# RWKV6 attention and an MLP mixer in one kernel: another written sequence for the whole program, and where the u-weighted grams of the first three units are masked

## The chip, the cores and the metric

The kernel runs on 1 core of one Trainium2 chip. The metric is the device time of one execution in microseconds (us). Three runs of the kernel before took 481.3, 478.45 and 478.63 us, the median is 478.63. The page and the trace show one further execution, which the hardware profiler took; its own time is given below.

## The reference

Attention in the RWKV6 form with batch 4, 8 heads, 768 steps and head size 48, then an MLP mixer over tokens (768 to 256 to 768) and over channels (384 to 1536 to 384). Everything is float32.

```
for t in range(S):                       # per batch and head, state is 48x48
    cur = outer(u * k[t], v[t])
    y[t] = r[t] @ (state + cur)
    state = w[t][:, None] * state + outer(k[t], v[t])

x = y as (4, 768, 384)
h = relu(x.T @ w_tok1) @ w_tok2          # over tokens
u = x + h.T
out = u + relu(u @ w_ch1) @ w_ch2        # over channels
```

## The kernel before

**Units.** The 768 steps of a batch are cut into 12 chunks of 64 (T), two chunks to a block of 128 rows, two blocks to a unit: three units per batch (UB), 12 units in all, 0 to 11. Units 0 to 2 are batch 0. A unit works through these pieces: `ends` (a scan on VectorE, DVE, over w, L435, into `to_end`), two range checks on ScalarE (ACT) that only set flags (L427, a pass over `to_end` into a tile `junk`), `keys` (L440), `begins` and `queries` (L443, L446), `tokens` (PE transposes the keys, L345, and ACT copies them, L350), `carry` (L365, outer products of keys and values), four state steps, each a scaling on ACT (`by`, L501, four instructions of two heads each) and an addition (`up`; in batch 0 a product by the identity on PE, L508, later on DVE, L516), `gram` (products of queries and keys inside a chunk), `mask` (L327, a masked copy from PSUM into the tile `at`), then `before` with `across` (L380, queries times the state), `seen` (L389 in the start, L392 later: ACT reads one column of the banks that `across` has filled), `after` with `within` (L401, `at` times values, added in the same banks, so it comes after `seen`) and `taken` (L407, ACT moves the result into the mixer's input).

**The u part.** The term `u * k` at a step itself needs the diagonal of a gram whose keys were scaled by u. In the first batch each unit makes it so: `own_u` scales the keys on ACT (L331), `own_gram` multiplies on PE (L315, into the two PSUM halves `gram`), and `own_put` on DVE multiplies the result by a mask of ones on the diagonal into `at`:

```
def own_put():
    for q, g in L.pop("own"):
        dve.tensor_mul(at[:, q], g, over_heads(on_diagonal, g.shape[1]))
```

`mask` of the same unit then writes the strictly lower part over it, so it must come after. Unit 3 does the same once for all later batches, whose units take that part by other means.

**Weights.** All four weight matrices arrive as 32-bit words and are converted piece by piece, 8 pieces in all: load, `plus` and `minus` on ACT (L264, L267), `lead` (L270), `two` (L273), `value` (L277) and `sum` (L281) on DVE. The first three pieces are the token weights, the others the channel weights `wch`.

**Mixer.** Batch 0 is mixed with the float32 weights directly: `hidden` (L947 and L669 in the exact form), `back` (L958), `turn` (a transpose, L969, copied by L974), up products (L993), down products (L1004). Batches 1 to 3 go through an exact scheme of split numbers: up products in three passes L772, L774 and L779, z by L754, L757 and L761 (ACT, ACT, DVE, with an addition L765 on GpSimd, POOL), and down products in three passes L790, L791 and L792. This needs the weights split: for the channel weights `up_part` on ACT (L579), `rest` on DVE (L583), `low_part` on ACT (L586), `store` of the parts into DRAM (L594), read back through a ring of SBUF buffers by `load_third` (L626). z shares its room with `wch`, from which the six stores of the up weights read. The tiles `spare` and `h_room` hold token weights in turn: `tok1_moves` (L704) writes what lies in them to DRAM (`kept`) and reloads it; `weight_form` (L711, L715) derives parts of them, `row_form` (L689) puts the mixer's rows there. `kept0` (L921) and `kept1` (L828) load the token weights of the next batch back from what was written.

**Order.** Nothing is left to a scheduler: every piece is a function, and PE, DVE, ACT and SP (whose queue issues most DMAs) take their instructions in the order in which the functions are called. For the start (units 0 to 2, the token weights, hidden layer of batch 0) that order is one long call `strict(...)` of functions; `behind(gate, f)` lets a load wait for the piece `gate`. The remainder is woven by `ORDER`, a string of digits: each digit takes the next piece of one of ten lists (0 the mixings, 1 and 2 joins and token parts, 3 hidden parts, 4 to 6 the units by i modulo 3, 7 loads, 8 the channel weights' conversion and splits, 9 the second hidden half):

```
pieces = interleaved(ORDER, first_mixing() + of_mixing[0], *of_mixing[1:4], *of_units, loads, weights_in_turn(), of_mixing[4])
```

Of the kernel before, what the change touches and what calls it, by code (L numbers as in the profile page):

```python
# [18 lines left out]
ALU = mybir.AluOpType  # L19
# [4 lines left out]
T = 64  # L24
C = S // 128
UC = 2
UB = C // UC
NU = B * UB
A = H // 2
# [20 lines left out]
MID = 3 * G // 4 * SEG1  # L50
ORDER = (
    "888008088078808800000888484440800840804080880808804844088488400448088408008888080080884808884040488844488888084840880880"
    "808840880808084448484008800080858808005000458500505588854545558485085848785005080558505855588400558085800005606068606846"
    "860600685786865658688606668086688566668868066800064869889466550048096660988848898089000484488044008000848080000018444141"
    "404040044004000000007000000404000440020000040550000050500000000000000005024200200045005020000555542000002004001224540105"
    "100550500055000750000000055050502000000500004500006624606000520000666506507606600506566660066600060066066606000000000000"
    "006405041104010500004006511611111661096012294296211041111044222990403443439223340234000004000010011000000400000007040000"
    "400040004004000400400000404000055000550000000000000000000005544000050000000000500014511000000000400000004555500545554000"
    "570550000450000000505550060000600066000506665000000665005600000000000066500001666656650661160651610000600006662106266212"
    "191166106100991111112002023393229933300002000001000110000000000000000000000000000000000000000000000000000000000000000000"  # L60
    "00000000000070001011000000000000000000000000000000000000000000000000000000000000000000000000000000000"
# [4 lines left out]
def rwkv6_then_mixer(  # L66
# [255 lines left out]
    def over_heads(mask, n=2):  # L322
        return mask.unsqueeze(1).unsqueeze(1).to_broadcast([128, n, X, T])
# [85 lines left out]
    def unit(i):  # L409
# [46 lines left out]
        def own_put():  # L456
            for q, g in L.pop("own"):
                dve.tensor_mul(at[:, q], g, over_heads(on_diagonal, g.shape[1]))
# [74 lines left out]
        def each(f, n):  # L533
            return [lambda m=m: f(m) for m in range(n)]

        return dict(ranges=each(ranges, 2), ends=ends, keys=keys, begins=begins, queries=queries, own_u=each(own_u, A),
# [481 lines left out]
    def attention_pieces(i):  # L1018
# [21 lines left out]
        small, large = (piece(e["ranges"][n], name, ("ACT", 1.4, k("ends"))) for n, name in enumerate(("small", "large")))  # L1040
# [34 lines left out]
    def interleaved(order, *streams):  # L1075
# [12 lines left out]
    e0, e1, e2 = (unit(i) for i in range(UB))  # L1088
    (_, p0, n0, lead0, two0, put0, add0), (_, p1, n1, lead1, two1, put1, add1), (_, p2, n2, lead2, two2, put2, add2) = to_tok
    _, p3, n3, lead3, two3, put3, _ = to_ch[0]  # L1090
    in_turn.update({pe.engine: None, dve.engine: None, act.engine: None, sp.engine: None})
    s0, s1, s2 = (e["updates"] for e in (e0, e1, e2))
    t0, t1, t2 = (e["scaled"] for e in (e0, e1, e2))
    strict(lambda: load_part(0, 1), masks, e0["ends"], e0["own_u"][0], e0["own_u"][1], e0["own_u"][2], e0["own_u"][3], e0["begins"],
           lambda: load_part(0, 0), e0["keys"], lambda: load_part(1, 1), e0["own_gram"], lambda: load_v(0), e0["ranges"][0], lambda: load_w(1),
           e0["tokens"], e0["queries"], e1["own_u"][0], e1["own_u"][1], e0["copied"][0], lambda: load_w(2), e0["gram"], e1["ends"], e0["copied"][1],
           lambda: load_part(1, 0), e0["carry"], e1["own_u"][2], s0[0], e0["own_put"], e1["own_u"][3], e0["ranges"][1], t0[1], s0[1],
# [248 lines left out]
```

## Time and profile before

| | us |
|---|---|
| median of three runs | 478.63 |
| the profiled execution, its own time | 478.31 |
| its span, first to last instruction | 476.5 |
| PE, matrix products, busy | 459.1 (96%) |
| PEld, weight loads of PE (beside products) | 409.6 (86%) |
| DVE busy | 344.6 (72%) |
| ACT busy | 265.8 (56%) |
| POOL busy | 54.2 (11%) |

The DMAs moved 85.34 MB, 179 GB/s in the mean. The granted clock of PE was 1.0 over the whole span.

Each row of a group names a line of the kernel, an engine, an operation, output<-input, and then a count and times. `L458` is line 458 of the kernel before. A bracket at a row's end, `[0.59 <-ACT raw L267]`, is the idle time of that engine ahead of the instruction and what ended it. Rows of the stretch view begin with from:to in us from the span's start. `SPq` is SP's DMA queue; a DMA row's last number is the median time from issue to landing. The numbers behind a slash, as in 1162/1194/1225, are the shortest, the mean and the longest duration in ns.

### The profile page before, as it was taken

How to read it: one execution, taken by the hardware profiler on the slowest of the kernel's cores; microseconds unless marked ns; L12 is line 12 of the kernel's file. 1: busy time of each engine (PE TensorE's matmuls, PEld its weight loads, DVE VectorE, ACT ScalarE, POOL GpSimd, SP SyncE). 2: the span in 40 equal slices, each digit the busy share in tenths (PEclk: the TensorE clock that was granted, in tenths of full speed). 3: DMA queues.
4: the chain of work that ended last, by engine and by line, in shares of the span. 5: the costliest groups of instructions: out<-in, count | busy, mean ns of one | idle time of the engine just before them, and what ended most of it. 6: DMA issues, size and time to landing. Idle time of an engine off the chain costs nothing.

```text
span 476.5 us, 12778 instructions
## 1 busy us (share of the span) xinstructions
PE 459.1 (96%) x5322; PEld 409.6 (86%) x5322; DVE 344.6 (72%) x495; ACT 265.8 (56%) x606; POOL 54.2 (11%) x58
## 2 busy tenths in 40 slices
PE   3899999999999999999999999999999999999996
PEld 2776588856797668999999999999999999999995
DVE  7998797679598877876897998685587885235341
ACT  6699876674678856453747385351837554134140
POOL 1000000000000001231302002130304003032130
PEclk9999999999999999999999999999999999999999
DMA  8865745573584556963888842754784513336331
GB/s 313 317 221 217 188 169 191 180 275 99 152 228 138 177 179 207 284 186 100 252 283 232 294 154 56 198 173 141 215 227 150 167 61 84 115 101 199 86 99 54
DMA packets 45055, 85.34 MB, mean 179 GB/s; under 512 B 4736, under 2 KB 37376, under 8 KB 44992
## 3 DMA queue, kind: packets, MB, share of 16 engines
q1 hardware_dynamic: 44704, 84.37, 56.3%
q8 instruction: 43, 0.70, 0.6%
q14 instruction: 20, 0.16, 0.1%
q10 hardware_dynamic: 288, 0.10, 0.1%
HBM read 72.65 MB, written 11.80 MB: 177 GB/s over the span
## 4 chain that ended last, share of the span: by engine, by line
PE 90%; ACT 4%; DVE 2%; DMA 2%; issue 1%; SPq 0%; DVEq 0%; ACTq 0%
PE bank L1004 10%; PE bank L772 8%; PE bank L779 8%; PE bank L774 8%; PE bank L790 8%; PE bank L792 8%; PE bank L791 8%; PE bank L993 7%; PE bank L667 3%; PE bank L989 3%; PE bank L726 3%; PE bank L315 2%; PE bank L401 2%; PE bank L380 2%; PE kv_ps L365 2%; PE bank L669 2%
## 5 line engine op out<-in xcount | busy, mean ns | idle before, releaser
L765 POOL TENSOR_TENSOR z_high<-z_high 128x384 fp32r<-128x384 f32 x48 | 52.9, 1107 | 406.7 <-DMA ring<-third 186.8
L754 ACT ACTIVATE z_high<-bank 128x384 fp32r<-128x384 f32 x48 | 23.5, 489 | 58.1 <-PE bank L779 57.7
L772 PE MATMUL bank<-x_forms,forms 128*128 128x384 f32 x216 | 50.3, 341 | 0.0
L779 PE MATMUL bank<-z_more,forms 128*128 128x384 f32 x216 | 50.1, 340 | 0.0
L774 PE MATMUL bank<-x_forms,ring 128*128 128x384 f32 x216 | 49.3, 337 | 0.0
L761 DVE SCALAR_TENSOR_TENSOR z_high<-bank,z_high 128x384 fp32r<-128x384 f32 x48 | 26.5, 554 | 31.4 <-ACT z_high L754 29.4
L1004 PE MATMUL bank<-wch,z 128*128 128x384 f32 x144 | 48.1, 488 | 0.0
L790 PE MATMUL bank<-forms,z_high 128*128 128x384 f32 x140 | 47.8, 342 | 0.0
L792 PE MATMUL bank<-forms,z_high 128*128 128x384 f32 x140 | 47.1, 337 | 0.0
L791 PE MATMUL bank<-ring,z_high 128*128 128x384 f32 x140 | 47.1, 337 | 0.0
L798 DVE SCALAR_TENSOR_TENSOR x<-bank,x 128x384 f32<-128x384 f32 x35 | 18.8, 553 | 39.0 <-PE bank L792 38.9
L1004 PEld LDWEIGHTS bank<-wch,z 128*128 128x128 f32 x144 | 26.8, 190 | 17.2
L501 ACT ACTIVATE before<-state,to_end 112x48 f32<-112x48 f32 x132 | 33.1, 324 | 13.0 <-DVE state L516 7.6
L779 PEld LDWEIGHTS bank<-z_more,forms 128*128 128x128 f32 x216 | 39.0, 188 | 0.1
L772 PEld LDWEIGHTS bank<-x_forms,forms 128*128 128x128 f32 x216 | 38.3, 188 | 0.5
L774 PEld LDWEIGHTS bank<-x_forms,ring 128*128 128x128 f32 x216 | 38.6, 188 | 0.0
L993 PE MATMUL bank<-xT,wch 128*128 128x256 f32 x144 | 32.0, 381 | 0.0
L993 PEld LDWEIGHTS bank<-xT,wch 128*128 128x128 f32 x144 | 27.0, 190 | 3.7
L757 ACT ACTIVATE z_high<-z_high 128x384 fp32r<-128x384 f32 x48 | 25.2, 525 | 3.5
L790 PEld LDWEIGHTS bank<-forms,z_high 128*128 128x128 f32 x140 | 26.3, 188 | 0.2
L791 PEld LDWEIGHTS bank<-ring,z_high 128*128 128x128 f32 x140 | 26.3, 188 | 0.0
L792 PEld LDWEIGHTS bank<-forms,z_high 128*128 128x128 f32 x140 | 26.3, 188 | 0.0
(243 smaller groups left out, 961.2 us busy)
## 6 DMA issues: line engine op xcount, KB each, us to landing
ring<-third SPq DMA_DIRECT2D x144, 192.0 KB, 3.4
raw<-in_words_ch_dram SPq DMA_DIRECT2D x8, 1023.8 KB, 4.8
rk<-in_rk_dram SPq DMA_DIRECT2D x36, 192.0 KB, 5.2
near<-in_near_dram SPq DMA_DIRECT2D x8, 768.0 KB, 5.0
w<-in_w_dram SPq DMA_DIRECT2D x10, 520.5 KB, 5.1
vt<-in_v_dram SPq DMA_DIRECT2D x12, 384.0 KB, 5.0
out_dram<-x SPq DMA_DIRECT2D x17, 192.0 KB, 2.8
third<-forms SPq DMA_DIRECT2D x12, 192.0 KB, 3.3
```

The source lines that it names most:

```text
L501: act.mul(t[:ROWS, a], state[bt, g][:ROWS, a], by_last(c, j)[:, a:a + 1])
L757: act.mul(z_form(jt, 2), z_form(jt, 0).bitcast(f32), 1.0 / BASE)
L761: dve.scalar_tensor_tensor(z_form(jt, 1), a, 0.0, z_form(jt, 0).bitcast(f32), op0=ALU.max, op1=ALU.subtract)
L765: pool.tensor_add(z_form(jt, 2), z_form(jt, 2).bitcast(f32), z_form(jt, 1).bitcast(f32))
L772: pe.matmul(a, up[m], xf(0)[:, m], start=m == 0, stop=False)
L774: pe.matmul(a, low[:, m], xf(1)[:, m], start=False, stop=False)
L779: pe.matmul(banks["a", jt], joint, xf(2)[:, m], start=False, stop=m == 2)
L790: pe.matmul(a, z[0], up, start=first, stop=False, skip_group_check=True)
L791: pe.matmul(a, z[1], held[bt, s, half, 1, jt], start=False, stop=False, skip_group_check=True)
L792: pe.matmul(a, z[2], joint, start=False, stop=last, skip_group_check=True)
L993: pe.matmul(ps, now["wch1"][:, jt // 4, m, ts(jt % 4, 128)], xT[:, m, ts(s, SEG)], start=(m == 0), stop=(m == DM // 128 - 1))
L1004: pe.matmul(ps, zs[s][:, jt, ts(n, 128)], now["wch2"][:, jt, :], start=(jt == 0), stop=(jt == NJ - 1))
```

## The change

Two things are changed, and both parts of the written order with them.

1. In units 0 to 2 `own_put` no longer multiplies on DVE. ACT copies each half of the gram from PSUM into `at`, and GpSimd then sets everything off the diagonal to zero there, in two `affine_select`s, one for each chunk of 64 rows. `mask` still comes after. Unit 3 keeps the multiplication.
2. The long call of the start is replaced by a string `FIRST` of names, which is read out in a loop (`0.own` is `own_gram`, `0.put` is `own_put`, `t0.load` the load of the first piece, `h0` a hidden product, `a<b` is `behind(b, a)`). It is another sequence of the same pieces. `ORDER` is replaced by another string, which gives another interleaving of the same lists.

```diff
+FIRST = (
+    "masks k0 0.own0 0.own1 0.own2 0.own3 r0 0.own 0.ends 0.small 0.large k1 1.own0 0.keys 0.begins 0.tokens 0.copied1 0.queries w1 v0 "
...
+    "2.up2 2.by3 t2.minus h3 2.before 2.seen c0.load<1.gram h5 t2.plus rk3 2.mask 2.after 2.taken1 h7 2.taken0 h4 h6 t1.sum 2.taken2 h9 "
+    "t2.lead t2.two t2.value c0.plus t2.sum c0.minus c0.lead c0.two c0.value c1.load<2.own c2.load<1.tokens h8 h11 h10 relu1 relu0 back0 "
+    "1.large 2.small 1.small 2.large w3<2.by3 v3"
+)
 ORDER = (
-    "888008088078808800000888484440800840804080880808804844088488400448088408008888080080884808884040488844488888084840880880"
...
+    "007888888888008088000088008404448888848808804008880008888000444444444888888880000444484840880448880004884484400080884500005"
...
@@
         def own_put():
             for q, g in L.pop("own"):
-                dve.tensor_mul(at[:, q], g, over_heads(on_diagonal, g.shape[1]))
+                if i < UB:
+                    act.copy(at[:, q], g)
+                    for j in range(2):
+                        of = at[ts(j, T), q]
+                        pool.affine_select(out=of, in_=of, compare_op=ALU.is_equal, fill=0.0, base=0,
+                                           pattern=[[0, 2], [0, X], [1, T]], channel_multiplier=-1)
+                else:
+                    dve.tensor_mul(at[:, q], g, over_heads(on_diagonal, g.shape[1]))
@@
-    strict(lambda: load_part(0, 1), masks, e0["ends"], e0["own_u"][0], e0["own_u"][1], e0["own_u"][2], e0["own_u"][3], e0["begins"],
...
-           h[10], add2, n3, behind(e1["tokens"], to_ch[2][0]), lead3, two3, rectified[0], h[9], h[11], rectified[1], e1["ranges"][0], e2["ranges"][1], e1["ranges"][1],
-           lambda: load_rk(3), put3, lambda: turned["back"](0))
...
+    for name in FIRST.split():
+        name, _, gate = name.partition("<")
+        strict(behind(named[gate], named[name]) if gate else named[name])
```

The lines of the changed kernel stand 11 lower than before up to about line 455 and 18 lower after that: L754 becomes L772, L711 L729, L594 L612, L626 L644, L392 L403, L401 L412.

What the new strings move is shown at three places, each before and with the change, the third on two engines.

**ACT, first z of batch 1 and the reloaded token weights** (z_high and z_more are parts of z, spare and h_room the reloaded tiles). Before:

```order
L754 ACTIVATE z_more<-bank_874 128x384
L754 ACTIVATE z_more<-bank_878 128x384
L501 ACTIVATE before<-state,to_end_93 112x48 x4
L427 ACTIVATE junk,flags<-to_end_93,least 112x1041
L754 ACTIVATE z_high<-bank_877 128x384
L757 ACTIVATE z_high<-z_high 128x384
L754 ACTIVATE z_high<-bank_874 128x384
L757 ACTIVATE z_high<-z_high 128x384
L754 ACTIVATE z_high<-bank_878 128x384
L757 ACTIVATE z_high<-z_high 128x384
L711 ACTIVATE spare<-spare 128x768
L711 ACTIVATE spare<-h_room 128x768
```

With the change:

```order
L772 ACTIVATE z_high<-bank_879 128x384
L775 ACTIVATE z_high<-z_high 128x384
L772 ACTIVATE z_more<-bank_882 128x384
L729 ACTIVATE spare<-spare 128x768
L729 ACTIVATE spare<-h_room 128x768
L519 ACTIVATE before<-state,to_end_93 112x48 x4
L772 ACTIVATE z_more<-bank_881 128x384
L519 ACTIVATE before<-state,to_end_93 112x48 x4
L733 ACTIVATE spare<-spare 128x768
```

The first two z_more rows before are the fifth and the sixth column of the first half. Both uses of the reloaded tiles (L711, now L729) stood behind the sixth and eight more rows of z and state; now they stand right behind the fifth column's z_more and ahead of the sixth's (z_more<-bank_881), with two rows of state scalings (L519) about it.

**SP, the six stores of the up weights** (third<-wch are the stores, ring<-third the loads of parts stored earlier). Before:

```order
L594 DMA third_3_140<-wch_127 128x2x384
L594 DMA third_4_141<-wch_127 128x2x384
L626 DMA ring_2005<-third_0_131 128x384 x2
L626 DMA ring_2005<-third_1_132 128x384 x2
L181 DMA w_90<-in_w_dram 128x1041
L594 DMA third_5_142<-wch_127 128x2x384
L626 DMA ring_2050<-third_2_133 128x384 x2
L626 DMA ring_2050<-third_0_137 128x384 x2
L626 DMA ring_2055<-third_1_138 128x384 x2
```

With the change:

```order
L612 DMA third_3_140<-wch_127 128x2x384
L644 DMA ring_1997<-third_0_131 128x384 x2
L644 DMA ring_1997<-third_1_132 128x384 x2
L612 DMA third_4_141<-wch_127 128x2x384
L192 DMA w_90<-in_w_dram 128x1041
L644 DMA ring_2059<-third_2_133 128x384 x2
L644 DMA ring_2059<-third_0_137 128x384 x2
L644 DMA ring_2064<-third_1_138 128x384 x2
L612 DMA third_5_142<-wch_127 128x2x384
L212 DMA vt<-in_v_dram 128x2x384
```

The sixth store (third_5) stood ahead of the loads of third_2_133, third_0_137 and third_1_138; now it stands behind these three rows of two loads each.

**DVE, the last conversion piece and unit 4** (wch is the converted weight; to_end_93 and rk_89 belong to unit 4, at_92 to unit 3). Before, beginning with the last piece's `lead`:

```order
L270 TENSOR_TENSOR raw<-raw 128x1024
L273 TENSOR_SCALAR raw<-raw 128x1024
L514 COPY state<-kv_ps 112x192
L277 SCALAR_TENSOR_TENSOR wch_127<-raw 128x1024
L281 TENSOR_TENSOR wch_127<-wch_127,raw 128x1024
L583 TENSOR_TENSOR forms_1208<-wch_126,forms_1208 128x768 x2
L516 TENSOR_TENSOR state<-before,kv_ps 112x192
L583 TENSOR_TENSOR forms_1208<-wch_126,forms_1208 128x768 x2
L327 COPY_PREDICATED at_92<-before_it,bank_877 128x512
L327 COPY_PREDICATED at_92<-before_it,bank_875 128x512
```

With the change:

```order
L338 COPY_PREDICATED at_92<-before_it,bank_883 128x512
L338 COPY_PREDICATED at_92<-before_it,bank_884 128x512
L281 TENSOR_TENSOR raw<-raw 128x1024
L534 TENSOR_TENSOR state<-before,kv_ps 112x192
L284 TENSOR_SCALAR raw<-raw 128x1024
L288 SCALAR_TENSOR_TENSOR wch_127<-raw 128x1024
L292 TENSOR_TENSOR wch_127<-wch_127,raw 128x1024
L442 MEMSET starts 112x17
L446 SCALAR_TENSOR_TENSOR to_end_93<-w_90,starts 112x1041
L447 RECIPROCAL starts<-to_end_93 112x16
L451 TENSOR_TENSOR rk_89<-rk_89,to_end_93 112x1024
L281 TENSOR_TENSOR raw<-raw 128x1024
```

Unit 3's mask (L327, now L338) stood behind the last conversion (L270 to L281) and its `rest` rows (L583); now it stands ahead of the conversion before that one, and unit 4's `ends` (L442 to L447) and `keys` (L451), which before followed later, stand ahead of the last conversion, whose `lead` is the last row here.

**ACT, the same place: `seen` of unit 3.** Before:

```order
L427 ACTIVATE junk,flags<-to_end_93,least 112x1041
L350 COPY kT<-bank_878 128x384
L350 COPY kT<-bank_873 128x384
L601 ACTIVATE forms_1208<-forms_1208 128x768
L586 ACTIVATE forms_1256<-forms_1208 128x768
L392 COPY seen<-bank_876 128x1
L392 COPY seen<-bank_874 128x1
```

With the change:

```order
L275 ACTIVATE raw<-raw,rebias 128x1024
L278 ACTIVATE raw<-raw,rebias 128x1024
L597 ACTIVATE forms_1242<-wch_126 128x768 x2
L438 ACTIVATE junk,flags<-to_end_93,least 112x1041
L403 COPY seen<-bank_880 128x1
L403 COPY seen<-bank_881 128x1
```

`seen` (L392, now L403) stood behind the third split of the weights (`low_part` L586, joining L601) and the copied keys; now it stands right behind the last conversion's `plus` and `minus` (L275, L278), two `up_part` (L597) and a range check (L438).

55 lines of the change are left out of this document (26 added, 29 removed), and 5 rows, old and new, of the table FIRST.

## The prediction

> **What bounds the kernel now.** I read the page's head first, then busy time by stretch, then what the matmul engine waits for once the start is over.
>
> ```profile
> span 476.5 us, 12778 instructions
> 6.00:48.00 42.00, 36.88 (x993) 28.96 (x994) 37.70 (x38) 33.89 (x89) 0.00 (x0) 1.00 0.76 276
> 48.00:60.00 12.00, 11.41 (x45) 6.86 (x44) 8.90 (x13) 10.88 (x17) 0.00 (x0) 1.00 0.73 175
> 60.00:180.00 120.00, 120.00 (x1276) 89.84 (x1275) 97.22 (x121) 81.78 (x174) 0.00 (x0) 1.00 0.55 180
> 212.00:290.00 78.00, 77.27 (x1118) 74.92 (x1117) 65.28 (x99) 45.04 (x110) 10.34 (x10) 1.00 0.67 205
> PE bank L969 <- ACT raw L267: 0.6, 1, 0.6
> PE bank L401 <- ACT seen L392: 0.6, 2, 0.3
> PE bank L401 <- issue: 0.5, 1, 0.5
> ```
>
> The columns of a stretch are its length, then busy time of PE, PE's weight loads, DVE, ACT and POOL. The last three rows are all of PE's waits from 58 us to the end. Two regimes show. Up to 48 us DVE (37.70 of 42) and ACT (33.89) set the pace, and from 48 to 60 ACT does (10.88 of 12). From 58 us on PE is full: its waits add up to 1.7 us in 418. So after 58 us the new order can win at most 1.7 us, and every microsecond by which something reaches PE late is added to the end, since no idle time is left in which to make it up. The sum below is made on the profiled execution, 478.3 us with a span of 476.5; the runs' median is 478.63. About 1%, or 4.8 us, is what a measurement of this kernel tells from no change.
>
> **The grams, units 0 to 2.** Three DVE multiplies go; ACT gains three copies of 128x1024 out of PSUM, GpSimd gains six selects of 64x1024.
>
> ```profile
> L458 DVE TENSOR_TENSOR at<-gram,u_rows x2: 1162/1194/1225, 13.9 to 28.5; 128x1024 f32<-128x1024 f32 x2
> 3.57 1.02 ACT L231 ACTIVATE kv_ps<-ident 32x1024 f32<-32x1024 f32 x1
> L223 POOL TENSOR_SCALAR_AFFINE_SELECT strictly<-strictly x2: 232/234/237, 1.4 to 1.7; 64x64 f32<-64x64 f32 x2
> masks.py:199 POOL TENSOR_SCALAR_AFFINE_SELECT ident<-ident 128x128 f32<-128x128 f32 x1 | 0.3, 293 | 0.0
> L765 POOL TENSOR_TENSOR z_high<-z_high x48: 1000/1014/2002, 188.7 to 460.6; 128x384 fp32r<-128x384 f32 x48
> ```
>
> DVE loses 3 x 1.2 = 3.6 us. An ACT instruction over 1024 columns took 1.02, so ACT gains 3 x 1.0 to 1.2, about 3.4. DVE falls from 37.7 to 34.1 and ACT rises from 33.9 to 37.3: the longer of the two is as long as before, and I cost this at 0. Its cover is ACT's free time in the first 48 us (8 us); without that it costs the whole 3.4, and if ACT's load does not count, it wins the 3.6 of DVE. The select has no row of its size. Its two rows differ by 59 ns for 64 more columns, so 1024 columns make 234 + 960 x 0.92 = 1.1 us, a pair 2.2; scaled from the two-input add (2.6 ns a column at 1014) a pair is 5.4. I take 2.2, since it is the same operation. In the new order DVE's masked copy of the unit waits for the pair, with the scan of unit 1 ahead of it as cover, so 2.2 costs nothing and anything beyond about 2.5 delays DVE.
>
> The longest L765 took 2002 against 1014 ns, so something on this chip can double a GpSimd instruction here. [...]
>
> **Hand-over at 48 to 60 us.** ACT now runs all four range checks (L427) in a row behind the second rectified hidden tile and ahead of the conversion of the next weights; before there were three.
>
> ```profile
> 50.90 1.17 ACT L427 ACTIVATE junk<-first,most 112x1041 uint8<-112x1041 f32 x1
> 52.19 1.17 ACT L427 ACTIVATE junk<-to_end,most 112x1041 uint8<-112x1041 f32 x1
> 58.72 0.52 PE L969 MATMUL bank<-ident,x 128*128 128x128 f32 x3 [0.59 <-ACT raw L267]
> ```
>
> One more is 52.19 - 50.90 = 1.3 us, on the chain conversion, DVE, x, transpose, for which PE already waits. Between 0 and 1.3; I take 0.9, as the hidden layer may end a little earlier.
>
> **Unit 3's attention, moved forward.** Its `across` and `within` stood on PE behind 40 down products of the first mixing; now 8 stand ahead of it and 6 between the two. `within` needs `seen` on ACT, which now stands behind two `up_part` (L579) and a range check. Those need the last weights' conversion, and on DVE unit 4's `ends` and `keys` and unit 3's mask have been moved ahead of that.
>
> ```profile
> 94.24 15.64 PE L1004 MATMUL bank<-wch,z 128*128 128x384 f32 x48
> 98.25 0.69 DVE L270 TENSOR_TENSOR raw<-raw 128x1024 int16<-128x1024 int16 x1 [1.87 <-ACT raw L267]
> 100.83 1.23 DVE L281 TENSOR_TENSOR wch<-wch,raw 128x1024 f32<-128x1024 f32 x1
> 102.15 3.78 ACT L579 ACTIVATE forms<-wch 128x768 fp32r<-128x768 f32 x5 [1.44 <-DVE wch L281]
> 106.78 1.33 DVE L327 COPY_PREDICATED at<-before_it,bank 128x512 f32<-128x512 uint8 x2
> 114.55 2.33 DVE L435 TENSOR_TENSOR_SCAN to_end<-w,starts 112x1041 f32<-112x1041 f32 x1
> 117.08 1.16 DVE L440 TENSOR_TENSOR rk<-rk,to_end 112x1024 f32<-112x1024 f32 x1
> 120.70 0.93 PE L345 MATMUL bank<-ident,rk 112*128 112x112 f32 x8
> 122.86 0.96 PE L380 MATMUL bank<-before,rk 48*64 48x48 f32 x42
> ```
>
> On the clock of before: ahead of 98.25 come 2.33 + 1.16 + 0.2 = 3.7 and 1.33, less the idle 1.87 that they fill, so +1.8 (the mask hidden too) to +3.1. The conversion then ends at 103.9 to 105.2 instead of 102.06. Two L579 at 3.78/5 = 0.76, a check of 1.17 and the copy put `seen` at 106.8 to 108.1. PE comes to `within` after 14 x 15.64/24 = 9.1 and the blocks L380 and L345 with 1.9: 105.2, or 106.1 with the 0.9 of the hand-over. It waits between 0.7 and 2.9; I take 1.5.
>
> **The last store of the up weights.** The first z of batch 1 (L754) writes where the six stores read from, so it needs the sixth landed. That store now stands on SP's queue behind six ring loads, which wait for the end of the last `back`; before it stood ahead of them.
>
> ```profile
> 183.52 3.17 SPq L626 DMA_DIRECT2D ring<-third  x7
> third<-wch SPq DMA_DIRECT2D x6, 384.0 KB, 3.3
> third<-wch SPq DMA_DIRECT2D x1, 384.0 KB, 5.6
> ```
>
> The second row is the median of the six stores, the third the one at 150 to 153 us with loads in front. Six issues at 3.17/7 = 0.45 put the store at 186.3, landed at 189.6 to 191.9. The first z takes 0.5 on ACT and 0.55 on DVE until its bank is free: 190.7 to 193.0. PE goes on with other columns and asks for that bank at the fifth: the sixth column ends at 194.84 (next fence: 194.30 + 0.54), a column takes 3 x 0.53 = 1.6, so the fifth begins at 191.7. Stall 0 to 1.3; I take 0.8.
>
> **The reload of the first token weights, bt 2.** SP issues the two reloads (L704) right behind the ring load of batch 1's sixth column; on ACT both uses (L711) and four state scalings now stand between the fifth and the sixth z. Before, ten ACT rows and 14 us lay between issue and use.
>
> ```profile
> 194.30 0.70 PE L779 MATMUL bank<-z_more,forms 128*128 128x384 f32 x3
> 195.43 1.00 ACT L501 ACTIVATE before<-state,to_end 112x48 f32<-112x48 f32 x4
> 200.08 0.34 PE L790 MATMUL bank<-forms,z_more 128*128 128x384 f32 x1
> 210.21 0.83 ACT L711 ACTIVATE spare<-spare 128x768 fp32r<-128x768 f32 x1
> spare<-kept SPq DMA_DIRECT2D x1, 384.0 KB, 7.0
> h_room<-kept SPq DMA_DIRECT2D x1, 384.0 KB, 7.3
> ```
>
> The ring load goes when L774 is done (194.3), the reloads at 194.8 and 195.2. With their own 7.3 the second lands at 202.5; L711 0.83, scalings 1.0 and the z 0.5 make 204.8. PE needs the sixth z ten products later, at 200.08: 4.7 late. With the 3.3 of a store of that size it is 0.6. I take 2.6, the middle, since what is in flight there (ring loads) is as before, but fewer.
>
> **The two write-backs and reloads, bt 1 to 2.** The write-backs of the token weights' low parts (L704), which stood 25 us ahead, now stand in one row with the loads `kept0` and `kept1`, which must wait for them. On ACT the first row form (L689), which overwrites what is written back, stands ahead of the sixth z, and L711 of the second weights ahead of `seen`.
>
> ```profile
> 262.63 0.68 PE L779 MATMUL bank<-z_more,forms 128*128 128x384 f32 x3
> 272.64 1.15 PE L380 MATMUL bank<-before,rk 48*64 48x48 f32 x64
> 264.09 0.54 ACT L689 ACTIVATE spare<-x 128x384 fp32r<-128x384 f32 x1
> kept<-spare SPq DMA_DIRECT2D x1, 384.0 KB, 6.1
> kept<-h_room SPq DMA_DIRECT2D x1, 384.0 KB, 7.9
> z_more<-kept SPq DMA_DIRECT2D x2, 384.0 KB, 7.4
> ```
>
> Write-backs at 263.1 and 263.6. The first landed (6.1) at 269.2, row form and z give 270.2, needed at 262.63 + 5.78 = 268.4: 1.8; with 3.3, none. The second landed at 271.5, `kept1` issued by 272.4 and landed by 279.8, two L711, one L715 and a row form: `seen` at 282.0. PE asks at 272.64 + 1.15 and six L667 (1.0): 274.8, so 7.2 late at the most, counting the 1.8; with 3.3 for each transfer 273.4, not late. I take 2.5 for both, nearer to the short end, since 6.1 to 7.9 are among the longest of their size.
>
> **Sum.** 0 + 0.9 + 1.5 + 0.8 + 2.6 + 2.5 = 8.3: 478.3 + 8.3 = 486.6 us, slower by 1.7%.
>
> **Rivals.** (1) *The transfers land in time.* At the short ends the terms are 0, 0.7, 0, 0.6, 0 and the hand-over 0: 1.3, or 479.6; up to 483.4 it is within 1%. For it: most stores took 3.3 or less. Against it: the four reload and write-back rows lie at 6.1 to 7.9. (2) *Faster.* If DVE alone sets the pace of the first 48 us, its 3.6 us are won in full, and if in addition the later PE waits (1.7) go and no transfer is late, 478.3 - 5.3 = 473.0. This decides when ACT's added 3.4 us fall into its 8 us of idle time and the places above cost less than 0.8 in sum. For it: 37.70 against 33.89; against it: three separate chains above would each have to be wrong. (3) *GpSimd at half speed.* Pairs of 4.3 to 5.4 us make DVE wait some 2 to 3 us in the start; with the terms above 486.6 + 2.5 = 489.1.
>
> **How the numbers follow.** The forecast 0.58, rival 1 0.22, rival 2 0.04 (0.03 of it beyond 1%), rival 3 0.16. Slower by over 1%: 0.58 + 0.16 = 0.74; within 1% 0.23; faster 0.03. The range goes from the middle of rival 1's lower half, 480.0, to 492.5: 6 above the forecast, as the long ends sum to 1.3 + 2.9 + 1.3 + 4.7 + 7.2 = 17.4, which can't all be reached, because a late PE makes the next transfer less late.
>
> **What would show it.** In the profile after: PE busy share down from 96%, with PE waits after 58 us of some 8 us instead of 1.7; PE waiting at the down product (line 808 there) behind ACT near 205 to 210 us, and ACT waiting for DMA at line 729; `within` (line 412) waiting for `seen` near 107; the four checks in a row ending near 54. Selects near 1.1 us, DVE's masked copies not waiting for POOL. Wrong it would be if ACT nowhere waits for a reload, or if the transposes at 59 us come earlier than 58.7 by more than 2 us.

## The result and the profile after

The changed kernel took 497.23 us in the median of four runs (495.62 to 502.51), the kernel before 478.54: a ratio of 1.0403, 95% interval 1.0307 to 1.0498. Forecast were 486.6 us and a range up to 492.5. The direction was right, the loss is more than twice as large. The profiled execution is the slowest of the four, 502.51 us with a span of 500.8, so the places below add up to some 24 us, not to the median's 18.7.

The head of the page and the granted clock in 40 slices:

```profile
span 500.8 us, 12788 instructions
PE 472.4 (94%) x5322; PEld 418.4 (84%) x5322; DVE 344.3 (69%) x492; ACT 269.6 (54%) x609; POOL 67.2 (13%) x64
PEclk9998999999999999989899979999999999999999
```

PE is idle for 28 us instead of 17, and it is also *busy* for 13.3 us more, with the same 5322 products. The clock row shows one source: in four places it is not 9. Finer stretches show how low it went (the third number from the right is the clock):

```profile
44.00:46.00 2.00, 2.00 (x34) 0.92 (x33) 1.79 (x3) 1.98 (x5) 0.00 (x0) 0.50 0.76 197
214.00:216.00 2.00, 2.00 (x8) 2.00 (x7) 1.97 (x4) 0.79 (x4) 0.00 (x0) 0.50 0.04 5
246.00:248.00 2.00, 2.00 (x8) 2.00 (x8) 2.00 (x4) 0.00 (x0) 0.00 (x0) 0.59 0.76 177
298.00:300.00 2.00, 2.00 (x14) 2.00 (x11) 1.04 (x3) 1.42 (x3) 0.00 (x0) 0.50 1.02 229
```

In the trace the clock stands at 0.5 for 3.41 us from 42.9, from 213.5 and from 244.2, and for 6.83 us from 295.4. PE was busy all the while, with one pause of 0.6 us. Products of 128x384 came 0.32 us apart in them (214 to 217 us), 0.17 to 0.18 behind them, so by my estimate about half of that is lost: 1.7 + 1.7 + 1.7 + 3.4 = 8.5 us. Before there was no such stretch between 22.6 us and the last product. (The 1.00 in the rows of the first 20 us or so is no measurement: the record of the clock begins at 22.6 us before and at 29.2 us in the changed kernel, and ahead of it the products ran slower. In the kernel before two products of L508 took 0.98 us at 19.0 and 0.58 us at 23.0.) PE's waits from 55 us on, over 1 us:

```profile
PE bank L412 <- ACT seen L403: 4.6, 3, 3.5
PE bank L326 <- issue: 1.8, 1, 1.8
PE bank L808 <- ACT z_more L772: 1.5, 1, 1.5
PE bank L987 <- DVE x L978: 1.3, 1, 1.3
```

And where they stand in PE's timeline, with ACT's rows that explain the first and the third:

```profile
113.29 1.19 PE L412 MATMUL bank<-vt,at 64*64 64x48 f32 x64 [0.85 <-ACT seen L403]
211.86 0.44 PE L808 MATMUL bank<-forms,z_more 128*128 128x384 f32 x1 [1.48 <-ACT z_more L772]
243.68 0.68 PE L326 MATMUL bank<-rk 48*64 48x64 f32 x29 [1.77 <-issue]
296.06 2.01 PE L412 MATMUL bank<-vt,at 64*64 64x48 f32 x64 [3.50 <-ACT seen L403]
...
208.72 0.84 ACT L729 ACTIVATE spare<-spare 128x768 fp32r<-128x768 f32 x1 [4.21 <-DMA spare<-kept]
283.88 0.53 ACT L707 ACTIVATE spare<-x 128x384 fp32r<-128x384 f32 x1 [4.10 <-DMA kept<-spare]
293.97 0.84 ACT L729 ACTIVATE z_high<-z_more 128x768 fp32r<-128x768 f32 x1 [1.81 <-DMA z_more<-kept]
```

The forecast's three DMA waits of ACT are there: the reload, the write-back under the row form, and the reload of the second token weights with `seen` behind it. Each stretch at half clock begins behind a PE wait: 1.50 at 39.7, 1.48 at 210.4, 1.77 at 241.9, 3.50 at 292.6. The sixth store, which the forecast counted too, held up the first z of batch 1 on ACT for 3.83 us, and PE waited 0.23 us for that z's bank:

```profile
200.27 0.49 ACT L772 ACTIVATE z_high<-bank 128x384 fp32r<-128x384 f32 x1 [3.83 <-DMA third<-wch]
201.41 0.80 PE L790 MATMUL bank<-x_forms,forms 128*128 128x384 f32 x3 [0.23 <-DVE z_high L779]
```

The start lost more than any one of these. The first `back` product on PE, before and after:

```profile
49.04 1.66 PE L958 MATMUL kv_ps<-h,wtok 128*128 128x384 f32 x4
```

```profile
55.44 1.56 PE L976 MATMUL kv_ps<-h,wtok 128*128 128x384 f32 x4 [0.58 <-ACT h L968]
```

It is 6.4 us late, and the first up product (59.08 before, 66.06 now) 7.0. PE's last product is 24.0 late, so another 17.0 come in between: waits of 0.85, 0.23, 1.48 + 0.30 (the products behind it), 1.77 and 3.50, together 8.1; three closings of the clock (stretches at half clock), 6.8; 2.1 that none of these shows.

### The profile page after: what moved, and what is told of

Read it like the earlier page. It is cut to its first block, busy times and chain, and to the rows that moved or that the text cites. A ratio compares the mean times of both kernels' runs of the same rounds, so it can differ in the third digit from the quotient of the medians.

```text
span 500.8 us, 12788 instructions
## 1 busy us (share of the span) xinstructions
PE 472.4 (94%) x5322; PEld 418.4 (84%) x5322; DVE 344.3 (69%) x492; ACT 269.6 (54%) x609; POOL 67.2 (13%) x64
## 4 chain that ended last, share of the span: by engine, by line
PE 70%; DMA 4%; DVE 2%; ACT 2%; issue 1%; SPq 0%; DVEq 0%; ACTq 0%
PE bank L1022 8%; PE bank L790 7%; PE bank L792 7%; PE bank L797 7%; PE bank L808 7%; PE bank L810 7%; PE bank L809 7%; PE bank L685 3%; PE bank L1007 3%; PE bank L744 3%; PE bank L412 2%; PE bank L687 2%; DMA z_more<-kept 2%; PE bank L753 2%; PE bank L391 2%; PE bank L326 1%
## 5 line engine op out<-in xcount | busy, mean ns | idle before, releaser
L783 POOL TENSOR_TENSOR z_high<-z_high 128x384 fp32r<-128x384 f32 x48 | 54.1, 1139 | 391.5 <-DVE z_high L779 164.8
L772 ACT ACTIVATE z_high<-bank 128x384 fp32r<-128x384 f32 x48 | 23.5, 489 | 61.7 <-PE bank L797 57.7
L790 PE MATMUL bank<-x_forms,forms 128*128 128x384 f32 x216 | 50.5, 342 | 0.2 <-DVE z_high L779 0.2
L808 PE MATMUL bank<-forms,z_high 128*128 128x384 f32 x140 | 48.6, 347 | 0.0
L1022 PE MATMUL bank<-wch,z 128*128 128x384 f32 x144 | 48.4, 490 | 0.0
L810 PE MATMUL bank<-forms,z_high 128*128 128x384 f32 x140 | 47.7, 340 | 0.0
L519 ACT ACTIVATE before<-state,to_end 112x48 f32<-112x48 f32 x132 | 33.2, 323 | 17.5 <-DVE state L534 15.4
L816 DVE SCALAR_TENSOR_TENSOR x<-bank,x 128x384 f32<-128x384 f32 x35 | 18.7, 551 | 31.1 <-PE bank L810 31.0
L809 PEld LDWEIGHTS bank<-ring,z_high 128*128 128x128 f32 x140 | 26.7, 191 | 0.0
L810 PEld LDWEIGHTS bank<-forms,z_high 128*128 128x128 f32 x140 | 26.7, 191 | 0.0
```

The costliest lines, as they stand in the source:

```text
L519: act.mul(t[:ROWS, a], state[bt, g][:ROWS, a], by_last(c, j)[:, a:a + 1])
L783: pool.tensor_add(z_form(jt, 2), z_form(jt, 2).bitcast(f32), z_form(jt, 1).bitcast(f32))
L790: pe.matmul(a, up[m], xf(0)[:, m], start=m == 0, stop=False)
L808: pe.matmul(a, z[0], up, start=first, stop=False, skip_group_check=True)
L809: pe.matmul(a, z[1], held[bt, s, half, 1, jt], start=False, stop=False, skip_group_check=True)
L810: pe.matmul(a, z[2], joint, start=False, stop=last, skip_group_check=True)
```

## The experiments

**The same kernel again.**

> The changed kernel once more, unaltered, to see which of its waits and clock dips come again. Theory 'gate' (PE waits of about 1.5 us and more put the granted clock to 0.5 for 3.4 us, which costs 1.7 us each): 494 to 500 us, again several stretches at 0.5, each right behind a PE wait of 1.4 us or more; where the waits differ, the stretches differ with them. Rival 'the dips are chance, not tied to waits': dips at other places, also where PE did not wait.

499.94 us (497.03 to 503.75), ratio 1.0428 (1.0387 to 1.0469). Behind 200 us PE waited at the same three places, with other lengths (for z_more 1.75, for instructions 3.0 at 243, for `seen` 2.5); in the start its longest wait was now 2.5 us for instructions at 48 us, not 1.5 for DVE at 39.7. ("For instructions" is my reading of `issue`, a wait for nothing that the profile shows.) The clock closed behind three of these four, at 50.5, 245.0 and 299.6, but not behind the 1.75 us at 212.5. Once, from 19.7 to 30.0 in the start, it stood at 0.5 again after having been full for 3.4 us. So the closings follow the waits, but a wait of 1.5 to 2 us closes it at one time and not at another. The runs of this kernel spread over 8 us, those of the kernel before over 5.

**Start and weave apart.** Three kernels: the multiplication back on DVE, the old start with the new weave, the new start with the old weave.

```diff
-                if i < UB:
+                if False:
                     act.copy(at[:, q], g)
```

> The changed kernel with both new strings, but the u-weighted grams of units 0 to 2 again multiplied on DVE; ACT copies and GpSimd selects go. Theory 'select' (the six selects took 1.1 to 3.2 us instead of the forecast 1.1, DVE's masked copies wait 2.9 us for them, two DVE rows of two SBUF inputs took 2.0 instead of 1.2): the start ends about 4.5 us earlier and the dip at 42 us goes, 490 to 492 us. Rival 'sequence' (the start is late because of the new sequence itself, with keys ahead of begins and the second check early): within 1.5 us of the changed kernel.

> The start as before (written list, grams on DVE), the weave behind it from the changed kernel. If what is lost adds up place by place: only the start's 7 us go, 488 to 491 us, and the waits for seen near 107 and 283 and for z_more near 205 stay, with dips of the clock behind the long ones. Rival 'the weave is late only because the start was': 478 to 481 us.

> The new start with copies on ACT and selects on GpSimd, the weave behind it as before. Adding up place by place: before plus the start's 7 us, 484 to 487 us, one dip of the clock near 42 us and none after 65 us. Rival 'the start is made up later': 478 to 481 us; rival 'the old weave can't bear a late start either': over 489 us with new PE waits after 65 us.

The old start with the new weave took 492.53 us, +14.2 on the 478.35 of before in those runs (ratio 1.0302, 1.0272 to 1.0331) and 1.5 above the range expected; the new start with the old weave 485.20, +6.9 (1.0131, 1.0100 to 1.0161). The sum, 21.0, is what the whole change cost there (499.94, +21.6): within the spread of these runs the two losses add up, and nothing of the start's is made up later.

With the multiplication on DVE it took 500.97 (ratio 1.0444, 1.0378 to 1.0510): no gain. So part 1 of the change is not the cause of the start's loss, although the selects were slow, DVE did wait for them, and two of its own rows ran longer beside them (the changed kernel's profile; the middle one of three durations is the median, not the mean):

```profile
L473 POOL TENSOR_SCALAR_AFFINE_SELECT at<-at x4: 1141/1686/3215, 13.9 to 36.7; 64x1024 f32<-64x1024 f32 x4
17.36 1.30 DVE L338 COPY_PREDICATED at<-before_it,gram 128x1024 f32<-128x1024 uint8 x1 [1.90 <-POOL at L473]
35.50 1.30 DVE L338 COPY_PREDICATED first<-before_it,gram 128x1024 f32<-128x1024 uint8 x1 [1.04 <-POOL first L473]
32.41 2.04 DVE L292 TENSOR_TENSOR wtok<-wtok,raw 128x1024 f32<-128x1024 f32 x1
39.04 1.98 DVE L457 TENSOR_TENSOR first<-first,x 112x1024 f32<-112x1024 f32 x1
```

In the kernel with the multiplication back, PE reached the first `back` product at 54.80, 0.6 us earlier than in the changed kernel's profile. What it met on the way, in its own timeline:

```profile
39.49 1.01 PE L412 MATMUL y_ps<-vt,first 64*64 64x48 f32 x50 [1.11 <-issue]
50.19 4.03 PE L965 MATMUL h_ps<-x,wtok 128*128 128x384 f32 x12 [2.43 <-issue]
```

These are stops inside a row of products, in which PE waits for no engine that the profile shows. In the old start with the new weave the waits are those of the weave alone, and there is one closing (207.6 to 211.1 us):

```profile
PE bank L401 <- ACT seen L392: 3.6, 3, 2.4
PE bank L790 <- ACT z_more L754: 2.6, 1, 2.6
PE bank L315 <- issue: 1.2, 1, 1.2
...
208.00:210.00 2.00, 2.00 (x7) 2.00 (x8) 1.60 (x4) 0.00 (x0) 0.00 (x0) 0.50 0.00 0
```

**The wait for `seen` filled with work.**

```diff
-            L["y"], L["see"] = across(r_, L["before"], half)
+            L["y"], L["see"] = across(r_, L["before"], half, 4 if i == 8 else 1)   # so many times over
```

> The changed kernel, but in unit 8 the products of queries and state (across) are computed four times over instead of once, each time from the start, so that PE has 3.5 us of work more in the place where it waited 2.2 to 3.5 us for seen (292 to 298 us). Theory 'gate' (a PE wait of that length puts the granted clock to 0.5 for 3.4 or 6.8 us): the extra work takes the place of the wait, no stretch at 0.5 between 285 and 310 us, median 1.7 to 3.4 us under the changed kernel's 497 to 500. Rival 'the dip has another cause': the dip stays there, the time is as before or up to 1.5 us longer. A third outcome, that PE stops in the row of 256 small products itself for want of instructions, would show as a wait on nothing (issue).

503.04 us (1.0539, 1.0504 to 1.0573): slower, not faster. The profile, of the quickest of the four runs (499.93), shows a part of it. Between 290 and 302 the clock was 1.00 throughout, as the first theory said, but the third outcome came as well:

```profile
PE bank L413 <- issue: 1.4, 1, 1.4
PE bank L392 <- issue: 1.2, 1, 1.2
```

PE stopped twice with nothing that the profile shows to wait for, so the filling made stops of its own, the first of them after 137 products of the lengthened row. The 2.6 us of these stops don't explain the whole of a median 3 to 6 us above the changed kernel's. For the gate this run decides little.

**Rows of small products apart.** At 240 us `carry`, `within` and `gram` stood in a row on PE; two groups of six down products, out of the next ones in line, were put between them (digits of `ORDER` moved).

> The changed kernel with two groups of six down products, out of the next ones in line, put between the blocks of small products around 240 us (carry of unit 7, within of unit 6, gram of unit 7, 64 each, which stood in a row). Theory 'code' (PE runs out of instructions there: 384 products and weight loads in 2.7 us, and a 16 KB block on the instruction queue that begins within 0.6 us of the gap in both traces): the wait on nothing at 242 us (1.8, 3.0 and 2.4 us in three profiles) falls below 0.5, the clock's stretch at 0.5 behind it goes, median 3 to 6 us under the changed kernel. Rival 'a buffer or a transfer that the trace doesn't name holds that gram': the wait stays at the gram, over 1 us.

The stop at 242 us is gone, and so is the closing behind it: between 235 and 300 us PE waits once, for `seen`.

```profile
PE bank L412 <- ACT seen L403: 3.4, 1, 3.4
```

The median, 498.08 (494.96 to 504.47; ratio 1.0414, 1.0328 to 1.0500), is no gain on 497.23 and 499.94, against 3 to 6 us expected; the profiled run, 495.40, is one of the two quickest. PE came earlier to `seen`, whose transfers did not, and in the other three runs the mean clock was 0.968 to 0.985. So it is shown that the unbroken row made that stop; what the stop costs in the median is not.

**A longer row, in the kernel before.**

```diff
+            L["y"], L["see"] = across(r_, L["before"], half, {4: 2, 5: 3, 7: 4, 8: 6, 10: 9, 11: 14}.get(i, 1))
```

> The kernel before, with across computed 2, 3, 4, 6, 9 and 14 times over in units 4, 5, 7, 8, 10 and 11 (64 small products each time, nothing to wait for). Theory 'code': from some length of the row on PE stops on nothing (issue) for about a microsecond or more, and again at about every further 16 KB of instructions; the short rows pass. Rival: PE goes through all rows without a gap, at 1.15 us for each 64. Time: 478.4 plus 32 times 1.15, 515 us, and more by the stops.

554.62 us in one execution, against 515 plus the stops. The stops add 18.3; the clock stood at half for 65 us besides. The six-fold row of unit 8 and, at 388 us, the nine-fold of unit 10, and the last piece of unit 11's fourteen-fold:

```profile
285.89 4.16 PE L381 MATMUL bank<-before,rk 48*64 48x48 f32 x266
292.75 3.44 PE L381 MATMUL bank<-before,rk 48*64 48x48 f32 x118 [2.70 <-issue]
388.36 3.94 PE L381 MATMUL bank<-before,rk 48*64 48x48 f32 x255
393.56 2.08 PE L381 MATMUL bank<-before,rk 48*64 48x48 f32 x128 [1.26 <-issue]
397.30 5.42 PE L381 MATMUL bank<-before,rk 48*64 48x48 f32 x193 [1.66 <-issue]
437.02 16.83 PE L381 MATMUL bank<-before,rk 48*64 48x48 f32 x579 [1.36 <-issue]
```

PE stops after some 260 small products here (as many weight loads beside them), after 160 in unit 7's row and 189 in unit 11's, and in the second row again after 128. The last pieces of both rows ran at half clock and did not stop: at 28 to 29 ns for each product (5.42 us for 193, 16.83 for 579) PE went on, at 16 (3.94 for 255) it stopped. The row of 192 in unit 5 passed, and at 240 us in the changed kernel 163 products in three blocks were enough.

Where the 128 come from can be counted. The kernel before ran 5322 products and as many weight loads, with 43 blocks of 16 KB on one instruction queue; this run has 2048 more of each and 59 blocks. So a block holds 256 instructions, 128 products with their loads. Behind 100 us there are nine such stops in this profile, and in all nine a block begins between 1.4 us ahead of the stop and 0.5 us into it. That alone proves little, since at 16 ns a row uses up a block about every 2 us; in the piece of 579, at half clock, five blocks came 3.2 to 4.1 us apart and PE did not stop.

The clock did something here that the changed kernel didn't show: it stayed at half from 397.3 for 10.2 us and from 434.9 for 23.9 us, and opened only some 5 us after the row of small products had ended (at 402.7 and 453.9). PE was idle for less than 8% of each 3.4 us in them but the first of the second. Why the clock did not open earlier is not shown.

**Three places of the weave mended.** The old start with the new weave, and in it: the uses of the reloaded tiles behind the sixth z; the write-back 40 pieces earlier, and the second token weights' first forms behind `within` of unit 8; the rows of small products apart, as above.

> The old start with the new weave (492.5 us), in which pieces are moved at three places: the two uses of the reloaded token weights stand behind the sixth z of batch 1 and its first down products; the write-back of the low parts stands 40 pieces earlier and the second token weights' first forms behind within of unit 8; and down products stand between carry, within and gram around 237 us. Theory 'three waits' (2.6 us for z_more, 2.4 for seen, 1.2 for code, and the clock at half behind the first make most of what the weave costs): those three waits go below 0.5 us each, no stretch at 0.5, 482 to 485 us; what stays above 478.3 is the wait for seen near 107 (0.9) and some 2 to 4 us that no wait shows. Rival 'each wait taken away only uncovers the next': over 488 us with new PE waits of over 1 us at other places.

483.68 us (483.00 to 484.77), ratio 1.0100 (1.0057 to 1.0143): +5.0 on before instead of +14.2: 9.2 us of the weave's loss came back, within the range expected, with no new wait over 1 us. What is left after 55 us, with a clock of 1.00 to the last product (the third row is again the first z, held up by the sixth store):

```profile
PE bank L401 <- ACT seen L392: 1.1, 2, 0.8
PE bank L969 <- DVE x L960: 0.6, 1, 0.6
PE bank L772 <- DVE z_high L761: 0.5, 1, 0.5
```

**The start, two more tries.** On the new start with the old weave: unit 2's four scalings by u moved ahead of unit 0's `seen`; and then in addition the multiplication back on DVE.

```diff
-... 1.keys 0.seen t0.minus 1.tokens k2<1.ends 2.own0 1.copied0 ... 2.own1 ... 2.own2 0.taken0 ... 2.own3 ...
+... k2<1.ends 0.before 1.keys 2.own0 2.own1 2.own2 2.own3 0.seen t0.minus 1.tokens 1.copied0 ...
```

> The new start with the weave of before (485.2 us), and in the start the four scalings of unit 2's keys by u moved ahead of unit 0's seen on ACT, where they stood behind its taken. Theory 'sequence' (DVE stood idle 2.8 us from 26 us on, until ACT had scaled unit 2's keys, which its own keys overwrite): that wait goes below 1 us, the start's end comes 2 to 3 us earlier, 482 to 483.5 us. Rival 'the start is late by other waits': within 1 us of 485.2.

> The new start with the weave of before, unit 2's scalings early, and in addition the u-weighted grams on DVE again (no copies on ACT, no selects). Theory 'two chains' (DVE waits for unit 2's scaling in one, for the selects in the other, so each alone brought nothing): 481 to 483 us. Rival 'code' (the start's end waits for instructions on PE, 2.4 us in the row of hidden products at 48 us and 1.4 at 39, whatever DVE does): 484 to 486 us and those two waits on nothing still there.

485.24 us (1.0166, 1.0132 to 1.0200) and 484.76 (1.0132, 1.0089 to 1.0175), against 485.20. The wait aimed at did go. `keys` of unit 2 on DVE in the changed kernel, and with the scalings early:

```profile
28.83 1.23 DVE L451 TENSOR_TENSOR first<-first 112x1024 f32<-112x1024 f32 x1 [2.77 <-ACT near L342]
```

```profile
26.18 1.16 DVE L451 TENSOR_TENSOR first<-first 112x1024 f32<-112x1024 f32 x1
```

DVE won 2.65 us there, and the time did not move: PE stood 2.5 us for instructions at 47 us in that profile. The rivals were right in both; the theory of two DVE chains fell.

**Unit 3's loads later.** The kernel of the run before, with `rk3` behind the loads of the channel weights.

> The kernel of the run before (new start, weave of before, unit 2's scalings early, grams on DVE; 484.8 us) with the four loads of unit 3's keys and queries issued behind the loads of the channel weights, as in the kernel before, instead of ahead of them at 32.6 us. Theory 'code behind data' (PE's instruction blocks come through the same DMA engines, which these loads keep full from 34 to 41 us, where before they were idle from 36 to 40): the stop for code at 38 us (0.9 to 1.5 us in every profile of the new start, none before) goes, 483 to 484 us. Rival 'the stops come from the sequence of the products alone': the stop stays, 484.5 to 485.5 us.

482.45 us (481.46 to 482.53), ratio 1.0083 (1.0069 to 1.0097): 2.3 less than 484.76 (2.0 when each is taken against its own runs of before), more than expected, but not by the mechanism expected. PE's stops in the run without and in the run with this move:

```profile
39.04 1.01 PE L412 MATMUL y_ps<-vt,first 64*64 64x48 f32 x50 [0.94 <-issue]
49.75 0.48 PE L965 MATMUL h_ps<-x,wtok 128*128 128x384 f32 x1 [2.44 <-issue]
```

```profile
39.12 1.01 PE L412 MATMUL y_ps<-vt,first 64*64 64x48 f32 x50 [0.80 <-issue]
48.74 1.45 PE L965 MATMUL h_ps<-x,wtok 128*128 128x384 f32 x4 [1.34 <-issue]
```

The stop at 38 us stayed, though the DMA engines now moved nothing from 37 to 40 us; the one at 47 us fell by 1.1. A third stop, 0.9 us at 262 us, which the profile without the move had, was not there with it. Data in the way of instructions is not what makes the first; for the others it stays open.

**The gate by itself.** The kernel before, with nine pauses of rising length in the middle of `within`:

```diff
+            if gap is not None and ca == X // 2 - 1:
+                pause(y, gap)      # ACT reads the half result, copies `gap` blocks of a constant, reads again
```

> The kernel before, with a pause in the middle of within of units 3 to 11: PE must wait until ACT has read its half result, copied a constant tile of 0, 2, 5, 8, 11, 14, 18, 24 and 30 blocks of 128 columns to nowhere and read again, so that PE's waits rise from about 0.7 to 4 us. Theory 'gate by windows' (the granted clock is set anew every 3.413 us on a grid that runs on; a window whose idle share is over about 0.5 is followed by one at 0.5; in the profiles so far all but one of 20 windows over 0.45 were, and none under 0.36): pauses up to 1.2 us never close the clock, those over 2.6 us always do, and between it depends on where the grid cuts them; each closing costs 1.7 us or 3.4. Rival 'only a wait of a whole window, 3.4 us, closes it': one or two closings, at the last two pauses. Time: 478.4 plus the pauses' 18 us and the closings.

507.42 us in one execution. Four of the pauses in PE's timeline, and the clock behind them:

```profile
228.42 0.67 PE L419 MATMUL bank<-vt,at 64*64 64x48 f32 x30 [1.37 <-ACT seen L403]
262.05 1.15 PE L419 MATMUL bank<-vt,at 64*64 64x48 f32 x32 [1.91 <-ACT seen L403]
284.36 0.73 PE L419 MATMUL bank<-vt,at 64*64 64x48 f32 x32 [2.18 <-ACT seen L403]
388.18 1.16 PE L419 MATMUL bank<-vt,at 64*64 64x48 f32 x32 [3.47 <-ACT seen L403]
...
228.00:232.00 4.00, 3.58 (x108) 3.48 (x109) 2.36 (x4) 1.21 (x5) 0.00 (x0) 1.00 0.08 19
262.00:265.00 3.00, 2.95 (x38) 2.86 (x39) 0.75 (x2) 2.91 (x10) 0.00 (x0) 0.50 0.24 62
285.00:289.00 4.00, 4.00 (x22) 3.89 (x17) 2.11 (x3) 3.43 (x6) 0.00 (x0) 0.61 0.22 81
```

All five pauses of 1.9 us and more (1.91, 2.18, 3.21, 3.47, 4.35) closed the clock, none of the four of 1.4 and less did. The rival, that a whole window of 3.4 us must be idle, is out.

## Why the prediction was wrong

The loss forecast was 0.9 for the start and 7.4 for the weave; the kernels that change one of them alone lost 6.9 and 14.2. So the start was missed by 6.0 and the weave by 6.8.

**The start's term failed.** The step was "the longer of the two is as long as before, and I cost this at 0". It compared busy sums of DVE and ACT (34.1 and 37.3 us), took the new sequence to fill the gaps as well as the old one, and left out the third engine of its own row, PE, busy for 36.88 of the 42 us. Measured: 6.4 us at the first `back` product where 0 was put, and +6.9 us alone. The hand-over's 0.9 was about right (7.0 less 6.4).

PE ran the same 996 products ahead of that `back` product in both profiles, but in the changed kernel it was busy with them for 41.7 us instead of 37.9 and idle for 2.6 us more. Half clock is what made them longer: the clock came full at 29.2 us instead of 22.6 and closed once more at 42.9. And PE had become the engine that sets the pace. In the chain of work that ended last, PE's own pieces make 13.2 of the first 46 us before, and 29.0 to 31.1 us in the four profiles of the new start with the old weave.

The grams' move is not the cause: with the multiplication back on DVE the medians were 500.97 against 499.94, and 484.76 against 485.24. Unit 2's scalings early, the grams on DVE and unit 3's loads late together brought +6.9 down to +4.0 (482.45 on 478.45). What is left differs from execution to execution, with PE's stops and the clock. Five profiles have the changed kernel's start unaltered, and their first `back` product came at 51.8, 52.7, 55.4, 55.6 and 57.1 us. In the two early ones the row of hidden products did not stop and the clock stayed full once it had come; in the three late ones the row stopped for 1.0 to 2.5 us and the clock, after it had first come full, was at half for another 3.4 to 13.7 us. The seventh 16 KB block of instructions began at 43.9 and 44.5 us in the two, at 48.3 to 48.4 in the three. Why it comes so late in some executions, and so what makes the start late in the first place, stays open.

**There was no term for the clock.** The 1.00 in the rows of before was read as a property of the kernel. In the profile after, closings cost 8.5 us, 6.8 of them behind 60 us.

**There was no term for instructions.** Three blocks of 64 small products had been put in a row at 240 us; PE stopped 1.8 to 3.0 us in every profile with that row and the new start, 1.2 with the old start, and not once it was broken up. The page of before had shown such stops (0.5 us, "issue"), and I read past them.

**The waits in the weave were right.** Forecast 1.5 for `seen` of unit 3, 0.8 for the sixth store, 2.6 for the reload, 2.5 for the write-backs, 7.4 in sum; measured 0.85, 0.23 (0.4 to 1.4 in the five other profiles of the new weave), 1.8 and 3.5, in sum 6.4. The signs named for the profile, ACT waiting for DMA at line 729 and `within` behind `seen`, were there; the four checks in a row ended at 60.4, not near 54, behind the late start. What the text missed is that a wait is paid more than once where it closes the clock: 1.48 us at 210 cost 1.7 more, 3.5 at 292 cost 3.4 more. Two of the sum's long and short ends are slips that change nothing: by its own terms the reload's short end is 0.7, not 0.6, and the write-backs' long end is 8.0, not 7.2 (279.8 and four ACT rows of 0.83, 0.83, 0.83 and 0.54 make 282.8).

**The rivals.** Of the rival with GpSimd at half speed the size was right: the three pairs of selects took 3.4, 4.1 and 4.4 us where 2.2 was put, and DVE waited 1.9 and 1.0. So the sign "Selects near 1.1 us, DVE's masked copies not waiting for POOL" did not come. The rival's pair of 4.3 us is the 2.2 times 2002/1014, the longest L765 against the median one: an estimate, since before has no select of this size. Single selects took 1.15 us with DVE idle and 1.14 on a masked copy, and 2.2 and 3.2 where a scan of two SBUF inputs ran beside them. The scans kept their 2.3 us, while the two other rows with two SBUF inputs shown above took 2.04 and 1.98 us instead of 1.2. The rival's price, put at 2.5, does not show: 0.6 at the first `back` product in one profile each, and no gain in the medians. The range's upper end was set by the long transfers, and nothing in it stood for PE itself becoming slower.

## What to carry to other kernels

In this kernel, which PE fills, a PE wait had up to two prices: its length, and the time lost at half clock behind it. In the changed kernel the clock closed behind windows of 3.4 us of which PE was idle for 0.44 to 0.85, and that cost 1.7 or 3.4 us; in rows of small products the clock stayed at half for up to 23.9 us. So waits of 1.5 us and more can be worth more than they look; a window in which PE was idle for less than 1.3 us (0.38 of it) never closed the clock here.

Rows of small products, each with its weight load, can make stops of their own: PE stopped after 128 to 266 of them at 16 ns each, with nothing that the profile shows to wait for. Larger products put between such blocks ended the stop at 240 us.

When a whole written order is replaced, busy sums of two engines say little: cost the start along its chain, piece by piece, with PE in it. Here the start was about a third of the loss (6.9 of 21).

## What the hardware showed

**The gate's windows.** In the changed kernel's trace the clock closes at 42.9, 213.5, 244.2 and 295.4 us; the differences, 170.7, 30.7 and 51.2 us, are 50, 9 and 15 times 3.413, and the stretches at one clock last 4, 1, 49, 1, 8, 1, 14, 2 and 58 times that, from 29.2 to 500.2 us. So in this trace it changes only on a grid that runs on. Laying that grid over all 14 profiles and taking PE's idle share of each window at full clock from its rows: of 22 windows over 0.515 idle all were followed by one at 0.5, of 16 between 0.38 and 0.515 six, of 1814 below 0.38 none (the two bounds were chosen to part these windows). In the changed kernel's profile the four windows ahead of these closings were idle for 0.44, 0.52, 0.52 and 0.85, and the idlest of the others at full clock, up to 490 us, for 0.37. So idle time of less than a window closed it at some places and not at others: in the changed kernel 1.48 us and the 0.30 behind it were enough, in one window (0.52 idle); in its repetition 1.75 us in one window (0.51) were not, nor were 2.4 us cut in two by the grid (the old start with the new weave, at 285 us).

**The first opening.** The full clock came for good at 22.6 us before, at 27 to 30 with the new start. How long PE's 996 products ahead of the first `back` take goes with it. Where the clock did not close again before that product, they took 35.4 us with the opening at 15.0 (the run with longer rows), 37.9 at 22.6, 39.4 at 26.7 and 40.6 at 28.8 (the last run of the start). Whether the end of the start moves with it depends on what sets the pace there: with the old start and the new weave, opening at 26.7, PE was busy 1.4 us longer but idle 1.0 less, and the first `back` product was 0.4 us late.
